# Group 0 in 64x64 tiles, convolution portions and weight copies in another order, first loads on other queues

## The chip, the cores and the metric

One core of one Trainium2 chip. The metric is the device time of one execution in microseconds (us); a run's figure is the median of several executions. The engines are TensorE (PE, matrix products into PSUM), VectorE (DVE), ScalarE (ACT), GpSimd (POOL) and SyncE (SP, which issues DMAs). ACT and POOL issue DMAs too. Each engine executes its own instructions in the order of the program; semaphores tie the engines together.

## The reference

```python
# x: (8, 4096, 192), weight: (8, 7), w_in: (192, 2048), w_out: (2048, 192)
w = exp(weight - max(weight)); w = w / (sum(w) + 1e-9)   # per head, over the 7 taps
out = einsum('hk,bskhg->bshg', w, windows of x padded by 6 zeros on the left)
x2 = out.reshape(32768, 192)
h = x2 @ w_in
return maximum(0.01 * h, h) @ w_out                       # float32
```

A causal convolution of 7 taps along the sequence, with one set of taps for each of 8 heads of 24 channels, and then two matrix products with a leaky ReLU between them.

## The kernel before, in words

**Layout.** The 192 channels are cut into three chunks of 64. Two sequences share a tile: partitions 0 to 63 hold a chunk of the one, 64 to 127 the same chunk of the other (index `e` in the code). xt is x transposed, channels on partitions and time along the row; yt is the convolved tile; ph (two PSUM buffers of the pool `psum_h`) is the first product; g is its leaky ReLU in bf16; po and acc are the second product. The pool `psum_o` has four banks, handed out in turn to everything with the tag "po": the transposes' ptr, the convolution's acc, po and acc2.

**Groups.** The main loop (L670) runs over groups of time steps. Groups 0 to 3 are 256 steps wide, all others 512. For each group, `mm1` (L488) makes the first product in steps u: 12 matmuls fill one ph tile (two blocks of 128 columns of w_in for a group of 256 steps), and one ACT activation (L515) takes it to g. Between the steps `mm2_slots` (L661) puts portions of the second product of an earlier group. Groups 0 to 3 have a 128-column stationary operand in `mm1` (two row tiles, 64*128 in the profile), later groups 64 columns (four tiles, 64*64). Group 0 has eight steps and no second product beside it; the first three slots of the second product (L525, six matmuls) stand ahead of group 1's first step.

**The convolution.** From group 2 on it is DVE's alone (`conv_jobs`, L209: one instruction for each chunk and tap, L222 and L228). For the first two groups part of it runs on PE: `pe_conv_jobs` (L244) multiplies xt by diagonal matrices, diag, which hold the taps, split into a high and a low bf16 part (`p`), in 64*64 tiles. For group 0, chunk 0 is high (hi) and low (low, taken out by ACT at L455) and a DVE join (L465), chunks 1 and 2 follow (taken out by ACT at L455 and DVE at L276). For group 1, chunks 0 and 2 are PE's, cut into three portions by CUTS and put behind steps u of group 0 (L700); DVE takes them out at L271 and L276 (`evac_0`, `evac_2`), and chunk 1 is DVE's (conv_1, seven instructions).

**The copies of w_in.** `w_in_of` (L328) needs each chunk's rows on both halves of the partitions. The DMA load brings 128 rows to slot 0 and 64 rows to slot 2; `spread_up` (L324) copies from the lower to the upper half, `spread_down` (L321) the other way. There are two parts n of w_in (steps u = 0 to 3 and u = 4 to 7 of group 0), each with a near and a far half (two steps each). Chunk 0 needs slot 0 copied up, chunk 1 slot 0 copied down, chunk 2 slot 2 copied up.

**The transposes.** x's rows for the first 256 steps come in by two DMAs (L142), are cast to bf16 (`cast_first`, L154) and transposed on PE. Those for the next two 256 steps (q = 1, 2: `x_rows`) are bf16 already: `transpose_first` (L162) multiplies by an identity in 128*64 tiles into one PSUM tile, ptr, and DVE copies it out (`evac_first`, L190). q = 1 stands within group 0's first product, ahead of chunk 2 (L502); q = 2 behind u = 6 (L706).

**The start.** w9 holds the taps: its maximum (L368, DVE), the exponential (L372, ACT), the split into bf16 parts (L379 to L382, DVE), a matmul with the selection matrix sel (L396) that spreads heads over channels, and the tile taps (L409, DVE), from which DVE makes six pieces of diag (L420).

## Time and profile before

| | us |
|---|---|
| three runs | 680.70, 680.72, 681.06; median 680.72 |
| profiled execution, first to last instruction (span) | 679.2 |
| PE busy | 674.9 |
| ACT busy | 517.6 |
| DVE busy | 481.2 |
| POOL busy | 147.4 |
| first L507 (group 0), first L507 of group 1 | 8.09, 17.37 |
| granted TensorE clock, mean | 1.000 |

Of the profiled execution the span is given, not the time around it; the median of the runs is 1.5 us longer than the span. A line of a timeline reads: start and length in us, engine, line of the code, operation, what it writes and reads, shape, number of instructions merged into the line, and in brackets the idle time before it with what ended it. A line of the chain of work reads: start, length, engine, tile written, line. DVE and ACT instructions overlap a little at their ends.

### The profile page before, as it was taken

Reading aid. Unit: us, or ns where it says so; the run is one execution under the profiler, and the core shown is the slowest. Engines: PE = TensorE matmul, PEld = TensorE weight load, DVE = VectorE, ACT = ScalarE, POOL = GpSimd, SP = SyncE. Lnnn points to the kernel's source line nnn. Section 1 sums busy time; section 2 is a strip of 40 time slices with the busy share of each in tenths; the row PEclk is TensorE's granted clock in tenths of the full one; section 3 lists DMA queues with packets and bytes.
Section 4 is the critical chain, followed back from the end, with each engine's and each line's share of the span. In section 5 each row is a group of like instructions: output and inputs, shape, how many; then the busy total and the mean of one; then the engine's idle time right before and its main releaser. Section 6 shows DMA issues by size and latency. Waiting matters only on the chain.

```text
span 679.2 us, 27092 instructions
## 1 busy us (share of the span) xinstructions
PE 674.9 (99%) x12442; PEld 446.3 (66%) x12442; DVE 481.2 (71%) x816; ACT 517.6 (76%) x601; POOL 147.4 (22%) x208
## 2 busy tenths in 40 slices
PE   9999999999999999999999999999999999999998
PEld 6997666666666666666666666666666666666667
DVE  7989477866768766778667687667786676876612
ACT  7899877777787777777777777778777777777781
POOL 8455221122211222211222112222022220000000
PEclk9999999999999999999999999999999999999999
DMA  9999755655737656556556566567365573321123
GB/s 149 99 119 104 52 85 83 84 64 67 96 74 93 76 54 86 84 85 86 66 63 92 80 92 78 56 83 94 73 87 69 60 96 71 72 56 33 34 49 94
DMA packets 213970, 53.27 MB, mean 78 GB/s; under 512 B 209312, under 2 KB 213536, under 8 KB 213856
## 3 DMA queue, kind: packets, MB, share of 16 engines
q0 software_dynamic: 98832, 13.97, 30.3%
q1 hardware_dynamic: 115008, 37.57, 28.0%
q8 instruction: 97, 1.59, 0.9%
q14 instruction: 17, 0.14, 0.1%
q10 hardware_dynamic: 16, 0.00, 0.0%
HBM read 28.31 MB, written 25.17 MB: 79 GB/s over the span
## 4 chain that ended last, share of the span: by engine, by line
PE 98%; DVE 1%; ACT 0%; issue 0%; ACTq 0%
PE ph L507 49%; PE acc L588 44%; PE po L525 5%; PE acc L259 0%; DVE diag L420 0%; PE ptr L167 0%; ACT L366 0%; ACTq L288 0%; DVE w_in L322 0%; DVE yt L465 0%; DVE o_sb L638 0%; DVE x_half L155 0%; ACT w L372 0%; DVE w_in L326 0%; ACT junk L366 0%
## 5 line engine op out<-in xcount | busy, mean ns | idle before, releaser
L515 ACT ACTIVATE g<-ph 128x1024 bf16<-128x1024 f32 x512 | 496.6, 1021 | 139.8 <-PE ph L507 139.6
L228 DVE SCALAR_TENSOR_TENSOR yt<-xt,wk,yt 128x512 bf16<-128x512 bf16 (+1 forms) x582 | 380.1, 715 | 0.2
L507 PE MATMUL ph<-yt,w_in 64*64 64x512 bf16 (+2 forms) x6048 | 377.5, 369 | 0.3 <-DVE yt L465 0.3
L588 PE MATMUL acc<-g,w_out 64*64 64x512 bf16 x5568 | 339.9, 376 | 0.0
L507 PEld LDWEIGHTS <-w_in 64*64 64x64 bf16 (+1 forms) x6048 | 229.7, 131 | 103.4 <-issue 1.1
L588 PEld LDWEIGHTS <-w_out 64*64 64x64 bf16 x5568 | 178.2, 118 | 118.8
L96 POOL DMA_DIRECT2D x_bf<-in_x_dram x180 | 133.9, 774 | 407.6 <-DMA xt<-x_bf 405.6
L610 DVE STREAM_TRANSPOSE o_t<-acc 128x512 f32<-128x512 f32 x87 | 72.9, 875 | 182.2 <-PE acc L588 182.2
L525 PE MATMUL po<-w_out,g 64*128 64x192 bf16 (+1 forms) x640 | 36.8, 243 | 0.0
L525 PEld LDWEIGHTS <-g 64*128 64x128 bf16 (+1 forms) x640 | 32.6, 95 | 3.2 <-issue 0.4
L222 DVE TENSOR_SCALAR yt<-xt,wk 128x512 bf16<-128x512 bf16 (+1 forms) x97 | 28.8, 320 | 2.4 <-DMA xt<-x_bf 2.4
L598 ACT COPY junk<-junk 128x1 f32<-128x1 f32 x58 | 11.1, 191 | 4.1
L638 DVE COPY o_sb<-po 128x192 f32<-128x192 f32 x8 | 2.8, 356 | 6.8 <-PE po L525 3.9
L638 ACT COPY o_sb<-po 128x192 f32<-128x192 f32 x16 | 5.1, 323 | 0.3
L259 PE MATMUL acc<-xt,diag 64*64 64x256 bf16 x126 | 4.7, 272 | 0.1
L149 POOL DMA_DIRECT2D x_half<-in_x_dram x6 | 4.3, 732 | 0.9 <-DMA w_in<-in_moe_w_in_dram 0.9
L259 PEld LDWEIGHTS <-diag 64*64 64x64 bf16 x140 | 3.7, 106 | 1.0 <-issue 0.4
L360 PE MATMUL warm<-const-bfloat16-1.0 128*128 128x512 bf16 (+2 forms) x8 | 3.3, 577 | 0.8 <-PEq L752 0.8
L145 POOL DMA_DIRECT2D x_rows<-in_x_dram x4 | 2.9, 746 | 0.0
L316 POOL DMA_DIRECT2D w_in<-in_moe_w_in_dram x5 | 2.9, 593 | 0.0
L360 PEld LDWEIGHTS <-const-bfloat16-1.0 128*128 128x128 bf16 x10 | 1.2, 128 | 2.2 <-issue 2.2
L326 DVE COPY w_in<-w_in 64x512 bf16<-64x512 bf16 (+1 forms) x7 | 2.3, 337 | 0.2
(52 smaller groups left out, 25.9 us busy)
## 6 DMA issues: line engine op xcount, KB each, us to landing
out_dram<-o_t SPq DMA_DIRECT2D x112, 192.0 KB, 4.7
x_bf<-in_x_dram POOLq DMA_DIRECT2D x180, 64.0 KB, 3.1
out_dram<-o_sb SPq DMA_DIRECT2D x8, 192.0 KB, 2.8
xt<-x_bf SPq DMA_TRANSPOSE x90, 3.2
w_out<-in_moe_w_out_dram POOLq DMA_DIRECT2D x2, 384.0 KB, 8.3
out_dram<-o_t SPq DMA_DIRECT2D x8, 96.0 KB, 2.4
out_dram<-o_sb SPq DMA_DIRECT2D x8, 96.0 KB, 1.7
w_in<-in_moe_w_in_dram POOLq DMA_DIRECT2D x2, 256.0 KB, 5.5
```

Of the source, the lines that this page charges most:

```text
L96: ins = nc.gpsimd.dma_start(out=t[:, c, :, e, :], in_=src[2 * rp + e, :, :, c * CH : (c + 1) * CH],)
L222: lambda s=src, d=dst, c=c: nc.vector.tensor_scalar_mul(d, s, wk[:, c, 0:1])
L228: lambda s=src, d=dst, c=c, k=k: nc.vector.scalar_tensor_tensor(out=d, in0=s, scalar=wk[:, c, k : k + 1], in1=d, op0=mybir.AluOpType.mult, ...
L259: lambda k=k, p=p, a=a, ps=ps, to=to, acc=accs[e]: nc.tensor.matmul(out=acc[to, :T], lhsT=diag[c][ps, p, k, :], rhs=xt[0][ps, c, a : a + T ...
L360: nc.tensor.matmul(out=to[:, 0:cols], lhsT=ones[:, 0:128], rhs=ones[:, 0:cols], start=True, stop=True,)
L507: nc.tensor.matmul(out=ph[m : m + M, e, i * T : (i + 1) * T], lhsT=w_in_of(f, e, c, m, m + M), rhs=y[ps, c, t0 : t0 + T], start=(c == chun ...
L515: act = nc.scalar.activation(out=g[blk][:, nf * u : nf * (u + 1), :, t0 : t0 + T], in_=ph.rearrange("p e (i t) -> p i e t", i=nf), func=my ...
L525: return nc.tensor.matmul(out=po[m], lhsT=g[b][ps, fc, e, s * 128 : (s + 1) * 128], rhs=w_out[ps, fc, :], start=start, stop=stop,)
L588: ins = nc.tensor.matmul(out=acc2[gi, r][e * CH : (e + 1) * CH, 0:T], lhsT=w_out_of(ps, fc, r), rhs=g[b][ps, fc, e, t0 : t0 + T], start=fi ...
L598: seal = nc.scalar.copy(out=junk, in_=junk)
L610: nc.vector.transpose(out=osb[gi, 0][:, 0 : T // GB, :, r], in_=acc2.pop((gi, r))[:, 0:T].rearrange("p (j k) -> p j k", k=GB),)
L638: ins = copy(out=o_sb[:, n % 2, :], in_=po.pop(n))
```

## The change

Nine edits, all of which act on the first 17 us.

1. The first product of group 0 uses 64-column stationary operands (64*64 tiles, 24 matmuls to a step); groups 1 to 3 keep 128.
2. `transpose_first` for q > 0 works in 64*64 tiles: 24 transposes of 64 columns into two PSUM tiles, one for each half r of the rows, each from the pool of four; `evac_first` copies out by r.
3. The portions of group 1's convolution on PE stand behind u = 1, 2, 3 (5, 5 and 4 jobs of each chunk) where they stood behind u = 1, 3, 5 (6, 5 and 3).
4. evac_0 and evac_2 follow u = 3 in place of u = 5, and the last three tap steps of conv_1 are put between and behind the two halves of evac_2. Four tap steps, not three, stand ahead of the copies of w_in's second part.
5. Those copies are six of half width, near ones first; they were four, two of them of full width.
6. spread_down of the first near half stands behind the join (L465), and spread_up of chunk 2 behind the scaling of chunk 2.
7. w9 is loaded through SP; x's first rows come in through ACT's queue (s = 0) and SP's (s = 1, behind w9). Before, w9 was on ACT's and both x loads on SP's.
8. The first load of w_in is issued by POOL between the two selects that make sel; it was issued behind both.
9. ACT casts all of x's second part (s = 1); DVE cast half of it. The memset of xt's halo (`new_xt(0)`) stands ahead of sel.

```diff
-    CUTS = {1: (0, 6), 3: (6, 11), 5: (11, 14)}
+    CUTS = {1: (0, 5), 2: (5, 10), 3: (10, 14)}
...
-            for s in range(HS):
-                nc.sync.dma_start(out=x_nat[q][:, :, s], in_=rows[:, :, s])
+            for s, queue in enumerate((nc.scalar, nc.sync)):
+                queue.dma_start(out=x_nat[q][:, :, s], in_=rows[:, :, s])
...
         if q:
-            t = psum_o.tile([128, HS, NCH, 128], BF16, name="ptr", tag="po")
+            ts = [
+                psum_o.tile([128, HS, NCH, CH], BF16, name=f"ptr{r}", tag="po")
+                for r in range(2)
+            ]
             for s, c in product(range(HS), range(NCH)):
-                for e in range(2):
+                for r, e in product(range(2), range(2)):
+                    ps = slice(r * CH, (r + 1) * CH)
                     nc.tensor.transpose(
-                        out=t[e * CH : (e + 1) * CH, s, c, :],
-                        in_=x_rows[q][:, e, s, c * CH : (c + 1) * CH],
-                        identity=ident,
+                        out=ts[r][e * CH : (e + 1) * CH, s, c, :],
+                        in_=x_rows[q][ps, e, s, c * CH : (c + 1) * CH],
+                        identity=ident[ps, ps],
                     )
...
+        if q:
+            dst = dst.rearrange("p c (s r k) -> p r s c k", s=HS, r=2)
+            for r, t in enumerate(ptr.pop(q)):
+                copies[r](out=dst[:, r], in_=t)
+            return
...
-    nc.scalar.dma_start(out=w9[:, 0:K], in_=weight)
+    nc.sync.dma_start(out=w9[:, 0:K], in_=weight)
     load_first(0)
...
+    new_xt(0)
...
             pattern=[[sign * CH, NCH], [sign, CH]],
         )
+        if sign == 1:
+            load_w_in(0, 0)
     nc.vector.tensor_copy(out=sel[:, :, 1, :], in_=sel[:, :, 0, :])
...
-    load_w_in(0, 0)
     ident = const_pool.tile([128, 128], BF16)
...
-    new_xt(0)
     cast_first(0, 0, nc.scalar.copy)
-    cast_first(0, 1, nc.scalar.copy, slice(0, 1))
-    cast_first(0, 1, nc.vector.tensor_copy, slice(1, 2))
+    cast_first(0, 1, nc.scalar.copy)
...
     spread_up(0, slice(0, 1), near)
-    spread_down(0, cols=near)
...
-    spread_up(0, slice(2, 3), near)
+    spread_down(0, cols=near)
     pe_1, evac_1 = pe_conv_jobs(groups[0], 1)
     pe_2, evac_2 = pe_conv_jobs(groups[0], 2, cross=True, accs=[acc_tile(), wps[:, 0]])
     run(pe_1, pe_2)
     evac_1(act_scale)
     evac_2(nc.vector.tensor_scalar_mul, act_scale)
+    spread_up(0, slice(2, 3), near)
     spread_up(0, slice(0, 1), far)
...
-                mm1(grp, u, 128 if i <= NSW else CH)
+                mm1(grp, u, 128 if 0 < i <= NSW else CH)
                 if i == 0 and u == 0:
                     evac_first(1, nc.vector.tensor_copy, nc.vector.tensor_copy)
                     spread_up(0, slice(2, 3), far)
                     conv_1 = conv_jobs(groups[1], (1,))
-                    run([conv_1[:3]])
-                    spread_down(1)
+                    run([conv_1[:4]])
                     spread_up(1, slice(0, 1), near)
-                    spread_up(1, slice(2, 3))
-                    run([conv_1[3:5]])
+                    spread_down(1, cols=near)
+                    spread_up(1, slice(2, 3), near)
+                    spread_down(1, cols=far)
                     spread_up(1, slice(0, 1), far)
-                    run([conv_1[5:]])
+                    spread_up(1, slice(2, 3), far)
...
-                if i == 0 and u == 5:
+                if i == 0 and u == 3:
                     evac_0(nc.vector.tensor_scalar_mul)
-                    evac_2(nc.vector.tensor_scalar_mul, nc.vector.tensor_scalar_mul)
+
+                    def after(n):
+                        def scale(*args):
+                            run([conv_1[n : n + 1]])
+                            nc.vector.tensor_scalar_mul(*args)
+
+                        return scale
+
+                    evac_2(after(4), after(5))
+                    run([conv_1[6:]])
```

More of the change, by code (lines that the diff above doesn't have):

```diff
@@ L163, in transpose_first @@
         if q:
-            t = psum_o.tile([128, HS, NCH, 128], BF16, name="ptr", tag="po")
+            ts = [
+                psum_o.tile([128, HS, NCH, CH], BF16, name=f"ptr{r}", tag="po")
+                for r in range(2)
+            ]
             for s, c in product(range(HS), range(NCH)):
-                for e in range(2):
+                for r, e in product(range(2), range(2)):
+                    ps = slice(r * CH, (r + 1) * CH)
                     nc.tensor.transpose(
-                        out=t[e * CH : (e + 1) * CH, s, c, :],
-                        in_=x_rows[q][:, e, s, c * CH : (c + 1) * CH],
-                        identity=ident,
+                        out=ts[r][e * CH : (e + 1) * CH, s, c, :],
+                        in_=x_rows[q][ps, e, s, c * CH : (c + 1) * CH],
+                        identity=ident[ps, ps],
                     )
-            ptr[q] = [t[:, s] for s in range(HS)]
+            ptr[q] = ts
             return
@@ L191, in evac_first @@
         dst = xt[0][:, :, HALO + q * HT : HALO + (q + 1) * HT]
+        if q:
[3 more added lines that the diff above has]
+            return
         dst = dst.rearrange("p c (s k) -> p s c k", s=HS)
         for s, t in enumerate(ptr.pop(q)):
-            for cs in (slice(0, 1), slice(1, NCH)) if q == 0 and s else (slice(0, NCH),):
+            for cs in (slice(0, 1), slice(1, NCH)) if s else (slice(0, NCH),):
                 copies[s](out=dst[:, s, cs], in_=t[:, cs])
@@ L295 @@
     nc.vector.memset(w9p, 0.0)
-    sel = const_pool.tile([128, NCH, 2, CH], BF16, name="sel")
-    nc.gpsimd.memset(sel[:, :, 0, :], 1.0)
-    for sign, off in ((1, 0), (-1, GRP - 1)):
-        nc.gpsimd.affine_select(
-            out=sel[:, :, 0, :], in_=sel[:, :, 0, :], compare_op=mybir.AluOpType.is_ge,
-            fill=0.0, base=off, channel_multiplier=-sign * GRP,
-            pattern=[[sign * CH, NCH], [sign, CH]],
-        )
-    nc.vector.tensor_copy(out=sel[:, :, 1, :], in_=sel[:, :, 0, :])
+    new_xt(0)
     NPW = 2
@@ L334, in w_in_of @@
         ]
-    load_w_in(0, 0)
+    sel = const_pool.tile([128, NCH, 2, CH], BF16, name="sel")
+    nc.gpsimd.memset(sel[:, :, 0, :], 1.0)
+    for sign, off in ((1, 0), (-1, GRP - 1)):
+        nc.gpsimd.affine_select(
+            out=sel[:, :, 0, :], in_=sel[:, :, 0, :], compare_op=mybir.AluOpType.is_ge,
+            fill=0.0, base=off, channel_multiplier=-sign * GRP,
+            pattern=[[sign * CH, NCH], [sign, CH]],
+        )
+        if sign == 1:
+            load_w_in(0, 0)
+    nc.vector.tensor_copy(out=sel[:, :, 1, :], in_=sel[:, :, 0, :])
     ident = const_pool.tile([128, 128], BF16)
```

## The prediction

> **What bounds the kernel now.** I read the share of each engine first, then the chain of work that ended last, then that chain in order of time, then the timelines of VectorE (DVE) and ScalarE (ACT) over the first 18 us.

> ```profile
> PE 674.9 (99%) x12442; PEld 446.3 (66%) x12442; DVE 481.2 (71%) x816; ACT 517.6 (76%) x601; POOL 147.4 (22%) x208
> ...
> PE 98%; DVE 1%; ACT 0%; issue 0%; ACTq 0%
> ```

> TensorE (PE) has 99% of the span and 98% of the chain. From 17.3 us to the end its pieces follow each other without a break, so whatever the change wins or loses before that point is passed on to the end in full. The change touches nothing behind it. The whole question is when PE starts the first product (mm1, L507) of group 1: 17.37 us in PE's timeline. The chain in order of time, start and length:

> ```profile
> 6.67 0.29 DVE w_in L326
> 6.96 0.01 issue
> 6.97 0.55 DVE w_in L322
> 7.52 0.03 issue
> 7.56 0.49 DVE yt L465
> 8.05 0.04 issue
> 8.09 0.63 PE ph L507 x8
> 8.72 0.46 PE ptr L167 x12
> 9.18 1.00 PE ph L507 x16
> 10.18 0.78 PE acc L259 x24
> 10.96 1.44 PE ph L507 x24
> 12.40 0.67 PE acc L259 x20
> 13.07 1.68 PE ph L507 x24
> 14.75 0.45 PE acc L259 x12
> ...
> 16.51 0.78 PE ph L507 x12
> ...
> 19.92 1.31 PE ph L507 x24
> ```

> Undisturbed, 24 products take 1.31 (last line), so 12 take 0.655. In group 0 the same 24 take 1.44, 16 take 1.00 instead of 0.87, 12 take 0.78. The convolution's matmuls start four at a time every 0.109, so 24, 20 and 12 of them are 0.655, 0.545 and 0.33; the chain charges 0.78, 0.67 and 0.45. Every passage between products (64*128), convolution (64*64) and transposes (128*64) costs 0.12 to 0.13. The line of 1.68 has 0.25 of waiting more (the list of waits gives 0.2 of it to the copy of w_in at L326).

> **The change, part by part.**

> *Fewer passages.* I count ten in the chain between 8.72 and 16.51 (the eleventh, at 8.09, lies under a wait). With products, convolution and transposes all in 64x64 tiles they vanish; one remains, ahead of group 1, whose products keep 64*128. Nine times 0.12 is 1.08. The products themselves cost no more: 24 of 64x64 on 256 columns are six rounds of four at 0.109, 0.655 again; L259 shows that rate with a fresh weight load for each matmul. No row shows 24 transposes of 64 columns; six rounds cost between 0.027 (half of a 128-column round) and 0.109 (a 256-column round) each. I take 0.055, the spacing of the transposes now (6 in 0.33): 0.33 as now, ends 0.16 and 0.65.

> [...]

> *Group 0 on PE and ACT.* Call C the start of the last third of group 0's first product (the third chunk): 9.11 now (first start in PE's timeline), so group 1 starts at C + 8.26. Without passages, from C: rest of the first product 0.22, product 0.655, cut 0.545, product 0.655, cut 0.545, product 0.655, cut 0.44, product 0.655: 4.37. Now no convolution is left between products five to eight, and ACT takes over: one activation (L515) takes 1.02, starts follow each other at 0.92, ph has two buffers, and PE waits 0.05 after a release.

> ```profile
> 9.57 1.94 ACT L515 ACTIVATE g<-ph 128x1024 bf16<-128x1024 f32 x2 [0.26 <-PE ph L507]
> 11.78 1.94 ACT L515 ACTIVATE g<-ph 128x1024 bf16<-128x1024 f32 x2 [0.28 <-PE ph L507]
> 14.13 2.98 ACT L515 ACTIVATE g<-ph 128x1024 bf16<-128x1024 f32 x3 [0.41 <-PE ph L507]
> ```

> ACT idles 0.2 to 0.4 at each return to PE, so PE set the pace; that is the slack PE can use before ACT stops it. Activation four starts at C+3.48 (end of the fourth product) and ends at 4.50, so product six starts at 4.55; activation five runs 4.57 to 5.59, product seven starts at 5.64 and ends at 6.30; transposes 0.33; product eight 6.63 to 7.28; one passage 0.12; three slots of the second product 0.25: group 1 at C+7.65. Of 1.08 + 0.25, ACT gives back about 0.7: the gain here is 0.6.

> *Where C goes.* Five edits.
> (1) GpSimd (POOL) issues w_in's first load, 0.69, between the two selects that make sel. sel is ready at 2.55 instead of 1.92. DVE's copy of sel moves from 1.95 to 2.59, and the maximum of the taps (2.19, 0.15) is queued behind it: 2.83 to 2.98. The exponential moves from 2.84 to 3.00: 0.16 late. Behind POOL's other DMA issues nothing moves; the load of w_in itself goes out 0.42 sooner (1.87 to 1.45).
> (2) DVE loses its half of the cast (L155, 3.96 to 4.32) and the memset of xt ahead of taps (L409, 4.23). With the exponential 0.16 late, the selection matmuls end at 4.16, and taps starts at about 4.20. The two cancel: diag as before, last one at 6.64.
> (3) ACT casts the whole second half: 0.51 instead of 0.35. The x loads land 2.6 after their issues at 0.81 and 1.32 on SP. The first goes to ACT's queue, where an issue took 0.60 against SP's 0.45; the second keeps its time, w9 taking the slot in front of it. w9 has room: its reader comes 0.64 later. Landing: as now at the one end, at the other 0.45 later, the last 0.45 of x's transfer shared with a w_in load that now starts 0.42 sooner. I take 0.15. Convolution then starts at about 5.3 instead of 5.15; but it now loses 0.11 waiting for the second diag (5.21), which will be there. The low part (L455, ending 7.21) moves by 0 to 0.1.
> [...]
> (4) spread_down (6.97, 0.55) leaves the path ahead of the join at L465. Late next is the low part at 7.21, so the join starts at 7.25 to 7.30 instead of 7.56 and ends at 7.75 to 7.80. Gain 0.27, but only for the first chunk.
> (5) Behind the join DVE now has spread_down, half of the third chunk's scaling (L276, 0.49) and spread_up (0.29), and the third chunk needs all three. spread_down is 0.55 in this place; L326 with the same shape is 0.29: both ends kept. With 0.03 between them C is 7.78 + 1.15 to 1.41 plus 0.05: 8.98 to 9.24. I take 9.1. So C stays: the 0.27 is paid back in the same queue.

> *DVE up to group 1.* Its timeline now:

> ```profile
> 13.45 1.00 DVE L228 SCALAR_TENSOR_TENSOR yt<-xt,wk,yt 128x256 bf16<-128x256 bf16 x2
> 14.48 0.29 DVE L326 COPY w_in<-w_in 64x512 bf16<-64x512 bf16 x1
> 14.80 1.00 DVE L228 SCALAR_TENSOR_TENSOR yt<-xt,wk,yt 128x256 bf16<-128x256 bf16 x2
> 15.72 0.48 DVE L271 TENSOR_SCALAR yt<-acc,rsum 128x256 bf16<-128x256 f32 x1
> 16.23 1.00 DVE L276 TENSOR_SCALAR yt<-acc,rsum 64x256 bf16<-64x256 f32 x2
> ```

> It ends at 17.23, just ahead of group 1 at 17.37, so it must come earlier too or nothing is won. New order from the join's end at 7.78: up to the spread of C 1.15 to 1.41; spread 0.29; two evacuations 0.65 (same elements in shorter runs; ends 0.65 and 1.0, the 0.48 of a PSUM read at L271 for each; I take 0.65); spread 0.34; four tap steps 0.32 + 3 x 0.52 = 1.88: 12.1 to 12.4. That is when w_in's second part lands (12.2, DVE idled 0.61 for it), so the idle goes. Six half spreads at 0.32 are 1.9 (four were 1.75 now): 14.0 to 14.3. Then L271, tap, L276, tap, L276, tap: six at 0.43 (independent neighbours overlap by 0.08, as L271 does after L228) to 0.52: 2.6 to 3.1. The end is 16.6 to 17.4, middle 17.0. Group 1's second chunk, 0.11 after its start, needs the last tap; its po banks need the second L276, 0.5 earlier (the transposes now take two of the four banks each, so the second po bank is the one that L276 empties).

> **Sum.** PE and ACT allow 9.1 + 7.65 = 16.75 (16.6 to 16.9); DVE allows 16.5 to 17.3, middle 16.9. The later counts: about 16.95 instead of 17.37, a gain of 0.42. The profile's span is 679.2; the median of the runs, 680.72, is 1.5 more, which lies around the span and stays. 680.72 - 0.42 = **680.3**.

> **Rivals.**
> *A, the forecast:* DVE's queue and ACT together leave 0.1 to 0.7 of the gain: 680.0 to 680.6. Chance 0.55. For it speaks that DVE ends 0.14 ahead of PE now.
> *B, all ends come out short:* spread_down 0.29, taps overlapping, x on time. C at 8.9, group 1 at 16.55: gain 0.8, 679.9. If the cuts' new places also let ACT run without any gap (eight at 0.92 from 9.4: 16.8 is its last end, two buffers behind PE) and w_in 0.4 sooner shortens DVE, 1.4: 679.3. Chance 0.23, of which 0.09 beyond 0.2%. Against it: the low part at 7.21 does not move.
> *C, passages go and nothing comes of it:* DVE's end stays at 17.2 to 17.4, the wait of PE on the last tap replaces the passages: 680.7. Chance 0.12.
> *D, slower:* one mechanism, x behind w_in. If the earlier w_in load takes the DMA engines from x for longer, every us of delay in the casts beyond the 0.11 of slack reaches the join, and through DVE's queue group 1. With 9.2 from join to last tap, group 1 is later than now once the join ends after 8.2, that is once x is 0.5 late. A whole w_in load ahead of half of x (landing 4.46 after issue against 2.6) is 1.9 late: 1.4 slower, 682.1; 1.0 late: 681.2. For it: DMA share 9 in the page's first slices. Against: x's packets come first. Chance 0.10, of which 0.04 beyond 0.2%.

> **Numbers.** 0.2% is 1.4 us, about what a measurement of this kernel can tell from no change. Faster by more: 0.09 (part of B). Slower by more: 0.04 (part of D). Within: 0.87. The range from 679.5 to 681.2 takes in A, C, most of B and half of D; it leaves out some 0.16.

> **What would show it.** In the chain after: no excess of 0.12 at group 0's passages, 12 products at 0.655; ACT's gaps ahead of L515 near nothing from the fifth activation on, PE's waits for it instead; the join near 7.3; C near 9.1; the third chunk behind L326; last tap near 17.0; group 1 near 16.95. A join after 8 or casts after 4.2 would make D; a last tap before 16.6 with PE there, B. Wrong altogether would be 64-column transposes over 0.65, or PE breaks behind group 1.

## The result and the profile after

The changed kernel took 684.38 us (median of 5 runs, 684.22 to 686.03) against 681.06 (median of 5, 680.70 to 681.41) for the kernel before beside it: a ratio of 1.0056, 95% interval 1.0045 to 1.0067. It is slower by 3.3 us, and the forecast was 0.4 faster. The span of the profiled execution went from 679.2 to 682.7.

The page of the changed kernel: busy time, the instruction queue q8 (taken for PE's by the count below), the chain by engine.

```profile
PE 676.5 (99%) x12562; PEld 448.1 (66%) x12562; DVE 481.6 (71%) x817; ACT 518.1 (76%) x601; POOL 147.5 (22%) x208
...
q8 instruction: 98, 1.61, 0.9%
...
PE 99%; issue 0%; ACT 0%; DVE 0%
```

PE is still the chain. Its busy time grew by 1.6, but PE should have been sooner and not busier. The chain in order of time shows where the rest is (start, length, what; "issue" is time in which the engine waited for nothing that the profile shows):

```profile
8.91 1.18 PE ph L514 x31
10.09 0.55 PE acc L268 x20
10.64 0.79 PE ph L514 x24
11.43 0.04 PE acc L268
11.48 0.47 issue
11.95 0.74 PE acc L268 x19
12.69 0.65 PE ph L514 x24
13.34 0.44 PE acc L268 x16
13.78 0.68 PE ph L514 x22
14.46 0.02 issue
14.49 1.03 ACT g L522
15.52 0.04 issue
15.56 0.81 PE ph L514 x21
16.38 1.50 issue
17.87 0.22 PE ph L514
...
18.39 1.27 PE ph L514 x22
...
23.42 1.31 PE ph L514 x24
```

Three things are to be read here. The passages are gone: a step of 24 products takes 0.65, a cut of 20 takes 0.55, one of 16 takes 0.44. Twice PE stands still with nothing to wait for: 0.47 at the second matmul of a convolution portion, 1.50 at the end of the seventh product. And a step of the same work takes 1.27 at 18.39 where it should take 0.65. The last line is the step that began at 19.92 before: it is 3.50 late.

The granted clock shows what the slow step is. By windows of the changed kernel (busy time and instructions by engine, then the granted clock, the DMA share and GB/s):

```profile
core 0: us, PE busy (x) PEld busy (x) DVE busy (x) ACT busy (x) POOL busy (x), PEclk, DMA share, GB/s
4.68:14.93 10.25, 9.58 (x306) 8.21 (x307) 9.28 (x30) 7.69 (x13) 9.52 (x16) 1.00 1.09 152
14.93:18.34 3.41, 1.70 (x69) 1.25 (x64) 2.27 (x5) 1.59 (x3) 0.83 (x3) 1.00 1.58 153
18.34:21.75 3.41, 3.41 (x54) 2.57 (x45) 3.26 (x11) 2.13 (x3) 3.41 (x5) 0.50 0.87 70
```

After a stretch of 3.41 us in which PE was busy for half the time, the clock is at 0.50 for the next 3.41, which loses 1.7.

The two stops, measured from start to start of the matmuls around them less the usual spacing, are 0.63 and 1.66. So 0.63 + 1.66 + 1.7 = 3.99 was lost, and the step is 3.50 late: the change without the stops is worth about -0.5, near the -0.42 of the forecast. This is a difference of measured numbers in one execution, not a time that some kernel ran in, and it takes it that each stop is passed on in full; that it falls so near the forecast may be chance.

**The theories.** *CODE*: PE's own instructions came late. The page before shows q8 as well:

```profile
q8 instruction: 97, 1.59, 0.9%
```

97 packets stand beside a PE that executes 12442 matmuls and as many weight loads: 24,884 / 97 is about 256 to a packet, 16,384 bytes by the record of one. The page names no engine for q8; that it brings PE's instructions is inferred from this count. By *CODE*, PE stops at an instruction whose packet is not there, and no semaphore shows it. Counted from the start, the two stops lie at PE's instructions 447 and 703, which are 256 apart. In 64x64 tiles group 0 issues 48 instructions in 0.655 us (24 matmuls, 24 weight loads), 73 to the us; in 64x128 tiles it is 24, or 37 to the us. From the third chunk of the first product to group 1 there are 524 instructions now and 324 before (262 and 162 matmuls, each with its weight load). *WAIT*, the rival: a wait that belongs to a place in the program (a buffer, a semaphore, a kind of tile) and that the profile doesn't name. *CLOCK*, beside either: a stop that leaves PE idle for long enough halves the clock for one stretch (0.50 for 3.41 us above).

The packets can be seen in the trace. DMA queues of the changed kernel in its window of 15.6 to 16.7 us (packets, MB, share of 16 engines):

```profile
q0 software_dynamic: 684, 0.18, 160.9%
q8 instruction: 1, 0.02, 5.5%
```

One instruction packet runs among 684 packets of POOL's loads; in the window from 10.7 to 15.6 there is none. By its record it runs from 15.67 to 16.63, 0.12 after the first half of w_out has landed (15.55). That distance is no rule: in the run with 40 more instructions below, the packet starts at 15.02 and this half lands at 15.88. PE had passed instruction 447 at 11.95 and goes on past 703 at 17.87.

### The profile page after: what moved, and what is told of

It is laid out like the page before. It is cut to its first block, busy times and chain, and to the rows that moved or that the text cites. A ratio compares the mean times of both kernels' runs of the same rounds, so it can differ in the third digit from the quotient of the medians.

```text
span 682.7 us, 27332 instructions
## 1 busy us (share of the span) xinstructions
PE 676.5 (99%) x12562; PEld 448.1 (66%) x12562; DVE 481.6 (71%) x817; ACT 518.1 (76%) x601; POOL 147.5 (22%) x208
## 4 chain that ended last, share of the span: by engine, by line
PE 99%; issue 0%; ACT 0%; DVE 0%
PE ph L514 49%; PE acc L595 44%; PE po L532 5%; PE acc L268 1%; PE warm L369 0%; ACT g L522 0%; ACT xt L204 0%; PE ptr L171 0%; ACT yt L461 0%; DVE o_sb L645 0%; PE ptr L185 0%; PE wps L405 0%; PE wps L268 0%
## 5 line engine op out<-in xcount | busy, mean ns | idle before, releaser
L514 PE MATMUL ph<-yt,w_in 64*64 64x512 bf16 (+3 forms) x6144 | 379.9, 369 | 1.9 <-issue 1.5
L325 DVE COPY w_in<-w_in 64x512 bf16<-64x512 bf16 x8 | 2.3, 312 | 0.2
```

Of the source, the lines that this page charges most:

```text
L514: nc.tensor.matmul(out=ph[m : m + M, e, i * T : (i + 1) * T], lhsT=w_in_of(f, e, c, m, m + M), rhs=y[ps, c, t0 : t0 + T], start=(c == chun ...
```

## The experiments

Each kernel was timed 5 to 11 times beside the kernel before; ratios are to it, with 95% intervals, and "span" times are those of the one profiled execution. L-numbers shift by a few lines between kernels.

**Products back to 128 columns, everything else changed.**

```diff
-                mm1(grp, u, 128 if 0 < i <= NSW else CH)
+                mm1(grp, u, 128 if i <= NSW else CH)
```

> The changed kernel with one edit undone: group 0's products keep 128-column operands (12 matmuls to a step), everything else as changed. Theory CODE: PE stops at 11.5 and 16.4 us because its instructions are not there yet; they come in packets of 16 KB (256 PE instructions), the stops lie 256 instructions apart, and the packet for the next 256 was usable 4.9 and 5.9 us after PE had entered the 256 before. Here group 0 issues half as many instructions for the products, the places of the two stops are reached near 13.0 and 19.5 us, after the packets (12.0 and 18.9): no stops, no fall of the clock, 680.5 to 681.2, level with before. Theory WAIT (a semaphore that the profile does not show: a copy of w_in, a bank, a load): the copies, banks and loads stand as in the changed kernel, so the stops stay, 683 to 685.

Measured: 681.59 (680.95 to 681.89), ratio 1.0006 [0.9997, 1.0014]. The loss is gone, and so are both stops; PE's timeline at the place of the first one:

```profile
10.00 0.74 PE L268 MATMUL acc<-xt,diag 64*64 64x256 bf16 x20
10.68 0.85 PE L514 MATMUL ph<-yt,w_in 64*128 64x256 bf16 x12
11.45 0.74 PE L268 MATMUL acc<-xt,diag 64*64 64x256 bf16 x20
12.13 0.84 PE L514 MATMUL ph<-yt,w_in 64*128 64x256 bf16 x12
```

The same convolution portion that stopped behind one matmul now runs its 20 at the usual rate. Edits 2 to 9 together make no difference that can be measured.

**The stops' place: 40 PE instructions more ahead of them.** The seven warm-up matmuls at the start become 27 shorter ones of the same total length.

```diff
-    warm(6, ST)
-    warm(1, 384)
+    warm(27, 128)
```

> The changed kernel with the seven warming matmuls ahead of the selection (3,456 columns) made into 27 of 128 columns (3,456 columns): 40 more PE instructions early, in the same PE time, and nothing changed behind them. Theory CODE: the stops stay at the same count of PE instructions and so come 40 instructions sooner in the program: the first not at the start of the convolution's second portion but about six matmuls into the product ahead of it, the second not at the end of the seventh product but at its beginning. Time 683 to 686. Theory WAIT: the stops stay at the same instructions of the program, the convolution's second portion and the end of the seventh product.

Measured: 684.32 (683.12 to 684.92), ratio 1.0047 [1.0035, 1.0059]. The chain:

```profile
10.74 0.29 PE ph L513 x5
11.03 0.14 issue
11.17 0.77 PE ph L513 x19
...
15.98 0.27 PE ph L513
16.25 1.13 issue
17.37 1.34 PE ph L513 x21
```

Both stops moved by 40 instructions towards the start of the program: from the second matmul of a convolution portion into the product ahead of it, from the end of the seventh product to its start. By count they are where they were, 447 and 703. That speaks for CODE and against WAIT: the stops moved with the count and left the places in the program where they had been.

**The start's edits alone (6 to 9), on the kernel before.**

```diff
-    nc.scalar.dma_start(out=w9[:, 0:K], in_=weight)
+    nc.sync.dma_start(out=w9[:, 0:K], in_=weight)
...
+        if sign == 1:
+            load_w_in(0, 0)
...
-    cast_first(0, 1, nc.scalar.copy, slice(0, 1))
-    cast_first(0, 1, nc.vector.tensor_copy, slice(1, 2))
+    cast_first(0, 1, nc.scalar.copy)
...
-    spread_up(0, slice(2, 3), near)
+    spread_down(0, cols=near)
```

> The kernel before with the edits of the start alone (w9 and x on other queues, the first w_in load between the selects, ACT's cast, the memset, the join ahead of spread_down, spread_up behind the scaling). Theory CODE: no more PE instructions than before, so no stops; the start pays nothing or 0.2, 680.7 to 681.2, level with before. Theory START (the loads' new order is to blame: what lands first has changed and something in group 0 waits for it): 683 to 685.

Measured: 681.24 (680.61 to 681.87), ratio 1.0002 [0.9993, 1.0011], no stops. The start neither wins nor loses.

**The tiles alone, on the kernel before.**

```diff
-                mm1(grp, u, 128 if i <= NSW else CH)
+                mm1(grp, u, 128 if 0 < i <= NSW else CH)
```

> The kernel before with 64-column operands in group 0's products alone (24 matmuls to a step), all else as before. Theory CODE: as many more instructions in the products as in the changed kernel; instruction 447 comes near 11.8 (packet near 12.2), 703 near 16.3 (packet near 18): one stop of 0.3 and one of 1.5 or so, and if the clock falls behind it 1.7 more: 682.5 to 685. Theory START or any theory that blames the transposes, the portions or the copies: 680.4 to 680.9, since eight passages fewer are left.

Measured: 684.54 (683.55 to 686.52), ratio 1.0054 [1.0042, 1.0065]: edit 1 is the whole loss. PE's timeline:

```profile
13.22 0.66 PE L507 MATMUL ph<-yt,w_in 64*64 64x256 bf16 x16 [1.29 <-issue]
...
17.01 0.41 PE L167 MATMUL ptr<-ident,x_rows 128*64 128x128 bf16 x8
18.59 0.30 PE L167 MATMUL ptr<-ident,x_rows 128*64 128x128 bf16 x4 [1.17 <-issue]
```

The second stop falls amid the transposes, which this kernel has unchanged, so the kind of tile doesn't make it either. The six runs show the clock's part: at a mean clock of 1.000 they took 683.55 and 683.57, at 0.999 684.34, the others 684.73 to 686.52. This profiled run (span 681.8, clock 1.000) had the stops, 1.45 and 1.3 from start to start, and no fall of the clock: it is 2.6 longer than before, about what the two stops last. (Counted as above they lie at 445 and 701 here, again 256 apart.)

**The packets sooner: w_out, x_half and x_bf loaded later.** The two loads of w_out, load_first(3) and load_x(2) are issued behind an activation of group 0, so that the packets would meet idle DMA engines.

```diff
-                mm1(grp, u, 128 if 0 < i <= NSW else CH)
+                act = mm1(grp, u, 128 if 0 < i <= NSW else CH)
+                if i == 0 and u == 2:
+                    late_loads(act)
```

> The changed kernel with the loads of w_out, of x's fourth part and of the next block of x held back until the activation of group 0's third product has run (about 12.5 us; they were issued from 7.9 us on). Theory LOAD (the instruction packet is late because the DMA engine that brings it is full of this kernel's own loads): at 11.9, when the second packet is asked for, only x_rows is still under way; the packet starts near 13 instead of 15.7, and the second stop falls from 1.50 to 0.5 or less; the first stays near 0.5, since the loads ahead of it are the same. 681.3 to 682.8. Theory FIXED (a packet takes five to six us whatever the load): both stops as they were, 683.5 to 685.

Measured: 683.12 (682.70 to 684.68), ratio 1.0034 [1.0022, 1.0046], above the expected range. PE's timeline (the profiled execution is the slowest of the five):

```profile
13.05 0.74 PE L268 MATMUL acc<-xt,diag 64*64 64x256 bf16 x19 [1.34 <-issue]
...
17.31 0.42 PE L171 MATMUL ptr<-ident,x_rows 64*64 64x64 bf16 x24
17.58 0.88 PE L519 MATMUL ph<-yt,w_in 64*64 64x256 bf16 x24
```

The second stop is gone: the packet started 1.13 after PE passed 447, where it took 3.7 in the changed kernel. The first stop, whose packet has loads ahead of it as before, was larger in this execution. And a new wait stands in this run's list of waits (total, times, longest):

```profile
PE ph L519 <- DVE yt L237: 2.0, 2, 1.7
```

The longer of the two ends at 49.4 us. The later loads bring DVE's convolution late, which the expectation had left out.

**The control for that: the kernel before with late loads alone.** The helper late_loads is the last experiment's.

```diff
-                mm1(grp, u, 128 if i <= NSW else CH)
+                act = mm1(grp, u, 128 if i <= NSW else CH)
+                if i == 0 and u == 2:
+                    late_loads(act)
```

> The kernel before with only the late loads, as the control for them. By CODE and LOAD the packets come sooner, where nothing waits for them; 680.6 to 681.3, level with before. Slower than 681.6 would mean that the late loads themselves hold something up (w_out ahead of the second product).

Measured: 682.85 (681.60 to 684.63), ratio 1.0027 [1.0015, 1.0039], where I expected no loss. PE waits for what now comes late:

```profile
PE po L530 <- DMA w_out<-in_moe_w_out_dram: 1.0, 2, 0.6
```

So the late loads cost some 1.8 by themselves, of which this wait is 1.0, and times with them are no price of the stops. What they do show is the packet: here it started at 14.38 instead of 16.50.

**Fewer instructions: 64 columns only in steps 1 to 3**, where the convolution's portions stand.

```diff
-                mm1(grp, u, 128 if 0 < i <= NSW else CH)
+                mm1(grp, u, CH if i > NSW or (i == 0 and 0 < u < 4) else 128)
```

> The changed kernel with 64-column operands only in the products of steps 1 to 3, between which the convolution's portions stand; steps 0 and 4 to 7 keep 128 columns: 120 fewer PE instructions, three to four passages more. By theory CODE instruction 447 lies 24 later in the program (first stop 0 to 0.2), and 703 at group 1's first product, near 17.1, against a packet near 17.9 (0.5 to 1.0). No fall of the clock. 681.0 to 682.3. By a theory that blames 64-column products or the clock as such: half way, 682.5 or so, stops where they were.

Measured: 682.58 (681.59 to 684.24), ratio 1.0023 [1.0014, 1.0031], above the expected range, and in two of the eleven executions the clock fell (0.997; 683.94 and 684.24), which I had ruled out. The second stop, which I had expected at a half to one us, is gone; the first, expected at 0.2 at most, is 0.77, because its packet started at 10.83 in this execution (9.70 in the changed kernel's). The first packet's start varies between 8.75 and 11.24 over the thirteen profiles; what moves it was not tested. The time alone would fit the rival (682.5), but the stop is not where the rival had it: it still lies at 447 by count, which is now behind 13 matmuls of the convolution's portion and not behind one.

**The same with late loads, held by step 2, and by step 1.** The second kernel has `u == 1` in the third line.

```diff
-                mm1(grp, u, 128 if 0 < i <= NSW else CH)
+                act = mm1(grp, u, CH if i > NSW or (i == 0 and 0 < u < 4) else 128)
+                if i == 0 and u == 2:
+                    late_loads(act)
```

> Both edits of the two runs above together. By CODE and LOAD no stop longer than 0.2 is left, and what the prediction reckoned for the tiles, less three or four passages of 0.12, shows: 680.3 to 681.0, against 681.0 of before. By FIXED: as the mixed tiles alone, 681.0 to 682.3.

Measured: 682.90 (682.61 to 683.76), ratio 1.0028 [1.0017, 1.0039], above the expected range. The first stop was 0.39 and there was no second, but PE's matmuls waited 0.3 for w_out and 0.3 for a convolution of DVE's that came late: waits that the late loads brought in the two runs above too.

> Mixed tiles as before (64 columns in steps 1 to 3 only), with the late loads held back only until the activation of group 0's second product (about 11.5 us, not 12.5 to 13). By CODE and LOAD the second packet, asked for near 12.7, still finds the DMA engines nearly free (start within 1.5 of the request, no second stop), and w_out now lands before the second product needs it: the first stop of 0.5 to 0.9 stays, the rest of the loss of the run with later loads goes. 681.2 to 682.2. If w_out's own data already stand ahead of the packet, it starts 3 us after the request and a second stop of up to 1 us is back: 682.3 to 683.5.

Measured: 682.42 (682.02 to 684.29), ratio 1.0025 [1.0014, 1.0035], stops of 0.79 and 0.28. With w_out issued sooner (at 11.69, against 13.44 by step 2) the second packet started at 16.00, 3.5 after PE passed 447, as without the late loads: the second of the two cases expected. No kernel of this study beat the one before.

**CLOCK by itself: the kernel before, PE held with the same code.** The first matmul of group 0's step 6 waits for the second half of evac_2; no instruction is added that computes.

```diff
+                    if hold is not None and n == e == m == 0:
+                        sync(ins, hold, "held")
...
-                    evac_2(nc.vector.tensor_scalar_mul, nc.vector.tensor_scalar_mul)
+                    held = evac_2(nc.vector.tensor_scalar_mul, nc.vector.tensor_scalar_mul)
```

> The kernel before with one added wait and no other instruction: the first matmul of group 0's step 6 waits for the second half of evac_2 (ends 17.2), so PE idles 2.2 us from 15.0 on, with all its instructions there. Theory CLOCK (an idle PE of that length is by itself answered with half the clock for 3.4 us, whatever made it idle): in part of the executions or all, mean clock 0.997 to 0.998 and 1.7 on top of the idle time: 683.0 with the clock kept, 684.5 to 685 with the fall. Theory IDLE (the fall has to do with the 64-column tiles or with the missing instructions): clock 1.000 throughout, 683.0 to 683.4.

Measured: 683.22 (683.01 to 684.86), ratio 1.0039 [1.0027, 1.0052]. Its PE timeline, at the wait:

```profile
17.68 0.84 PE L508 MATMUL ph<-yt,w_in 64*128 64x256 bf16 x12 [2.09 <-DVE yt L276]
```

And its windows, columns as above:

```profile
14.50:18.00 3.50, 1.41 (x29) 0.94 (x27) 2.99 (x7) 1.94 (x2) 2.05 (x3) 1.00 1.50 165
18.00:22.00 4.00, 4.00 (x52) 2.99 (x50) 2.62 (x9) 2.05 (x2) 3.72 (x5) 0.57 1.06 82
```

PE's next instructions had long come: it passes 703 only at 24.4, and that packet had ended at 17.74. An ordinary wait of 2.1 did to the clock what the stop did, in some executions: 683.01, 683.14 and 683.22 at a mean clock of 1.000, 684.30 and 684.86 at 0.998 and less. A fall added 1.1 to 1.9.

**The same, waiting for evac_0 only.**

```diff
-                    evac_0(nc.vector.tensor_scalar_mul)
+                    held = evac_0(nc.vector.tensor_scalar_mul)
```

> The same, waiting for evac_0 (ends 16.2): PE idles 1.1 us, not 2.2. By CLOCK the clock is kept or falls in a few executions only, since the idle part of any 3.4 us is a third: 681.7 to 682.3, up to 1.7 more where it falls. By IDLE 681.7 to 682.3.

Measured: 681.89 (681.31 to 682.77), ratio 1.0013 [1.0004, 1.0021], at a clock of 1.000 in all eleven runs. PE's timeline at the wait:

```profile
16.27 0.84 PE L507 MATMUL ph<-yt,w_in 64*128 64x256 bf16 x12 [1.06 <-DVE yt L271]
```

The wait of 1.06 cost 0.8 by the medians (681.89 against 681.12), and the clock stayed.

The length of the idle time alone does not decide, though. In two other profiles (40 more instructions, then late loads; columns as above):

```profile
13.91:17.32 3.41, 1.88 (x45) 1.14 (x45) 3.24 (x9) 2.24 (x3) 2.31 (x4) 1.00 1.44 184
17.32:20.74 3.42, 3.37 (x77) 2.81 (x79) 2.16 (x7) 1.24 (x2) 2.71 (x4) 0.50 1.00 82
...
46.28:49.69 3.41, 1.67 (x36) 1.30 (x32) 3.41 (x6) 1.71 (x3) 0.12 (x1) 1.00 1.44 133
49.69:53.11 3.42, 3.17 (x51) 2.46 (x50) 1.46 (x4) 2.23 (x3) 0.09 (x1) 1.00 0.69 91
```

The first fell behind a stop of 1.28 and a wait for ACT of 0.46 just before it; the second kept its clock behind a wait of 1.7 with PE busy for less. What sets a fall off is left open.

**The packets of all these but the two held kernels, side by side.** Times in us by the trace's DMA and PE records; "pass" is when PE goes on at that instruction.

| kernel | packet of 447 to 702 | PE passes 447 (stop) | packet of 703 on | PE passes 703 (stop) |
|---|---|---|---|---|
| before | 9.94 to 10.92 | 13.8 (none) | 16.50 to 17.48 | 20.4 (none) |
| changed | 9.70 to 10.68 | 11.95 (0.63) | 15.67 to 16.63 | 17.87 (1.66) |
| products at 128 | 9.87 to 10.87 | 12.9 (none) | 15.83 to 16.78 | 19.6 (none) |
| 40 more ahead | 8.75 to 9.86 | 11.17 (0.3) | 15.02 to 15.91 | 17.37 (1.28) |
| tiles alone | 10.78 to 11.73 | 13.22 (1.45) | 16.34 to 17.27 | 18.59 (1.3) |
| late loads | 10.66 to 11.61 | 13.05 (1.5) | 14.18 to 15.61 | 17.2 (none) |
| steps 1 to 3 | 10.83 to 11.78 | 13.03 (0.77) | 16.27 to 17.20 | 18.7 (none) |
| steps 1 to 3, late by step 2 | 10.43 to 11.39 | 12.72 (0.39) | 13.77 to 14.94 | 18.7 (none) |
| steps 1 to 3, late by step 1 | 10.13 to 11.11 | 12.49 (0.79) | 16.00 to 16.98 | 18.41 (0.28) |
| start alone | 10.84 to 11.85 | 14.0 (none) | 17.14 to 18.1 | 20.5 (none) |
| before, late loads | 10.10 to 11.07 | 14.1 (none) | 14.38 to 15.48 | 22.0 (none) |

Wherever PE stopped in these profiles, it went on 1.2 to 1.5 after the packet's end. Wherever it arrived later than that, there was no stop; the nearest are steps 1 to 3 and late loads at 703, 1.5 and 1.6 after it. In kernels that stopped at 447, the second packet follows the passing of 447 by 3.1 to 3.9, and by 1.1 where the loads are held by step 2 (and the changed kernel's third packet, at 18.91, follows the passing of 703 by 1.0). In kernels without a stop there it follows by 2.7 to 3.1, and by 0.3 with late loads; PE's sequencer was perhaps ahead of the matmuls there, which no record shows. That PE asks for a packet when it enters the one before it is inferred from these distances; no record shows the request.

The count of about 256 instructions to a packet and the stops 256 apart agree. From the passing of 447 to the passing of 703 the changed kernel needed 5.9 us, of which 1.66 were the stop; the kernel before needed 6.6 (13.8 to 20.4) and did not stop.

## Why the prediction was wrong, point by point

**The step that failed** is "The products themselves cost no more: 24 of 64x64 on 256 columns are six rounds of four at 0.109, 0.655 again". The rate is right: 0.65 in the chain. What was costed at nothing is that the products have twice as many instructions, in a stretch where each 256 of them come in a packet among this kernel's first loads (q0 had 160.9% of the 16 engines from 15.6 to 16.7, while the second packet ran). The convolution's rows, which I took as the proof, show 73 instructions to the us for 0.3 to 0.65 at a time; the change keeps that rate up almost without a break. In the profiled execution the stops cost 0.63 and 1.66, and behind the second one the clock falls, which loses 1.7.

**Passages.** Gone, as forecast. The 24 transposes of 64 columns take 0.27, from start to start with late loads (17.31 to 17.58), where 64x64 products follow; the estimate was 0.33. In steps 1 to 3 it is 0.32 (17.21 to 17.53), with a passage to 64x128 products behind them.

**The join and C.** The join was forecast at 7.25 to 7.30, C at 9.1 (9.00 now, from when the products of the third chunk follow each other; two of them started at 8.68 and 8.74), the last tap's end at 17.0. DVE's timeline:

```profile
7.24 0.48 DVE L471 SCALAR_TENSOR_TENSOR yt<-acc,rsum,low 128x256 bf16<-128x256 f32 x1 [0.47 <-ACT low L461]
7.76 0.35 DVE L321 COPY w_in<-w_in 64x512 bf16<-64x512 bf16 x1
...
16.84 0.48 DVE L237 SCALAR_TENSOR_TENSOR yt<-xt,wk,yt 128x256 bf16<-128x256 bf16 x1
```

The join is at 7.24, with the low part as what it waits for, as said; spread_down behind it is 0.35, between the bounds of 0.29 and 0.55; the last tap ends at 17.32, in the range of 16.6 to 17.4. DVE was not what held group 1.

**ACT.** The forecast had the fourth activation at C + 3.48 and ACT's pace from there. Its timeline:

```profile
9.48 3.02 ACT L522 ACTIVATE g<-ph 128x1024 bf16<-128x1024 f32 x3
13.39 3.03 ACT L522 ACTIVATE g<-ph 128x1024 bf16<-128x1024 f32 x3 [0.89 <-PE ph L514]
18.25 1.02 ACT L522 ACTIVATE g<-ph 128x1024 bf16<-128x1024 f32 x1 [1.82 <-PE ph L514]
```

The first three have no gap. The fourth comes at 13.39, where C + 3.48 is 12.5 with the measured C: the first stop, 0.63, is most of that; the other 0.3 was not traced. Behind it the chain does show ACT's 1.03 at 14.49 between two products, the wait that the sum had.

**The start, and rival D.** x came 0.16 and 0.17 sooner in this execution (3.26, 3.77; in other profiles with these edits 3.33 to 3.50 and 3.85 to 4.10, before 3.42 and 3.94), not up to 0.45 later: its issue took 0.43 on ACT's queue, where the row I went by, w9's issue there, had 0.60. D's mechanism, x behind w_in, did not occur, and the start alone gave 1.0002. The kernel is slower for a cause that stood in none of the rivals.

**Group 1** was forecast at 16.95 and starts at 20.04: the two stops, and half of the 1.7 us of low clock that lie ahead of it, are 3.1. From the end of the low clock on the delay is passed on in full, 3.5 in the span.

**What stays open.** No kernel here has all of group 0 in 64 columns without a stop, so the 0.4 to 0.5 that the change would win without the stops is seen only as a difference, and never as a time. Why the first packet starts between 8.75 and 11.24 was not tried. In the changed kernel the runs don't part by the clock as cleanly as elsewhere (684.22 at 1.000, 684.38 at 0.998), so the split of 3.3 into stops and clock is that of the profiled execution. The run of 684.22 lost 3.2 with the clock whole, so its stops, or something else in it, were longer.

## What to carry to other kernels

Before smaller tiles are put on PE, count its instructions, weight loads too, over the stretch, and set 256 of them against the time that an instruction packet needs while loads run: here 5.9 us from one stop to the next in the changed kernel, 6.2 with 40 instructions more ahead (11.17 to 17.37). In this stretch, with q0 at 117.3% of the 16 engines from 10.7 to 15.6 us and 160.9% from 15.6 to 16.7, 73 instructions to the us in products and convolution alike were not kept up; with 37 in the products and 73 in the convolution's portions there was no stop. The idle times of PE put down to "issue" that came back 256 instructions later (447 and 703) were late code here; where such a distance shows, look for the packet on the instruction queue, and for the loads that run beside it. A PE stop of 1.66 us cost 1.7 more through the clock in the profiled execution, where a wait of 1.1 left the clock at 1.000 in eleven executions.
